# Hardware DMA for all of q, k and v, and x of three batches transposed by DMA, in a windowed-attention and gMLP kernel

## The chip, the core and the metric

The kernel runs on one core of a Trainium2 chip. A core has five engines that run side by side, each with its own in-order queue of instructions: TensorE (PE, matrix products and transposes, results in PSUM), VectorE (DVE), ScalarE (ACT), GpSimd (POOL) and SyncE (SP), which computes nothing and only issues transfers. PE's weight loads are shown as an engine of their own, PEld. Sixteen DMA engines move data between the chip's main memory and the on-chip memory SBUF. A transfer is issued from the queue of SP, of ACT (both "hardware DMA": the data keep their type) or of POOL ("software DMA", which can change the type on the way, here f32 to bf16). Engines wait for one another through semaphores.

The metric is the device time of one execution in microseconds (us).

## The reference

Attention with a sliding window of 128 and four sink tokens, for 4 batches of 8 heads, 768 positions and 64 columns, and on its result x a gMLP block with a spatial gate:

```python
scores = scale * np.matmul(q, k.transpose(0, 1, 3, 2))
is_sink = pos[None, :] < int(n_sink)                 # n_sink = 4
rel = pos[:, None] - pos[None, :]
in_window = (rel >= 0) & (rel < int(window))         # window = 128
scores = np.where(is_sink | in_window, scores, -1000000000.0)
a = softmax(scores); attn_out = np.matmul(a, v)

x = attn_out.transpose(0, 2, 1, 3).reshape(B, S, H * D)      # 4 x 768 x 512
h = gelu_tanh(x @ w_in)                              # w_in 512 x 1024
u, v = h[..., :512], h[..., 512:]
v_n = (v - mean) / np.sqrt(var + 1e-06) * g_ln       # over the 512 columns
v_s = np.einsum('ts,bsd->btd', w_sg, v_n) + b_sg[None, :, None]
return x + (u * v_s) @ w_out                         # w_out 512 x 512
```

All inputs and the output are f32; the products are made in bf16.

## The kernel before

All work is cut into steps. A step is a small function named by two or three letters with the indices of its batch, head pair and part, and it issues one instruction or a few, always on the same engine. The string STEPS (line 15) lists every step in one order, and the loop at line 475 issues them in that order; each engine's queue so holds its own steps in the order of the list and takes them strictly one after another. Semaphores between engines follow from the tiles that the steps read and write. Buffers are rings of a few tiles: a step that takes the next tile of a ring waits until the last reader of that tile is done.

The steps of the attention, for batch b and head pair p (four pairs):

- LQ, LK (lines 165, 168): load q and k of a pair, 384 KB each, from SP. LV (171): load v from POOL by software DMA, already as bf16, in pieces of 64 elements of one position; two heads at a time for batch 0, four after that.
- CQ, CK (182, 185): cast q and k to bf16 on POOL. TQ, TK (257): transpose them on PE, six matmuls each, to PSUM; EQ (263) on DVE and EK (268) on ACT copy them to SBUF.
- QK (292): scores of a group g of two 128-row tiles (three groups per pair) on PE. EX (304): exp on ACT. MK (309): the window mask, on DVE by a product with a mask tile for g = 0 and for all of batch 0, else on POOL by two selections (lines 318 and 322). KS, SK, SX: the sink tokens.
- AV (329): product with v on PE, in two halves of three row tiles; NR (354): division by the sum of weights on DVE, written to x_sb, one half of x for one pair.

The steps of the gMLP for a batch:

- XT (363): transpose 128 columns of x on PE, six matmuls; XE (369): copy them on ACT to xT, so that xT holds x transposed. Four of each for a batch, XT.b.p after both NR of pair p.
- MV (375): x @ w_in, second half of the columns, two row tiles jj at a time, eight matmuls; GV: gelu on ACT; BN, RS, Z (387 to 418): the normalization. BN runs on DVE; RS is four short steps on POOL (399 to 403); Z runs on ACT for row tiles below ZACT = 4 and on DVE for the rest.
- MU (420): first half of the columns, transposed, eight matmuls for each of four parts; GU: gelu on ACT.
- WT, WE (432, 438): w_sg transposed on PE, once. SP (441): the spatial product, six matmuls for each half hf and part dc; GT (448): times g, plus b, on DVE; GM (453): times u, on POOL.
- OU (457): product with w_out, four matmuls for each of six row tiles; RA (464): plus x, on DVE, into one of four ot buffers; ST (467): store from SP.

The remaining loads: LW (188, two halves), LWS and LWO load w_in, w_sg and w_out from POOL by software DMA as bf16. LC (199) loads the first four rows of v, g and b_sg in ten small transfers from SP, as its first.

Steps of three batches overlap: while PE works on the gMLP of batch b, the attention of b + 1 runs between, and q, k and v of b + 2 are loaded. The attention of batch 0 stands alone at the start, the gMLP of batch 3 alone at the end.

Of the kernel before, what the change touches and what calls it, by code (L numbers as in the profile page):

```python
# [20 lines left out]
LQ.1.1 LK.1.1 AV.0.1.0 EQ.0.3 EX.0.2.0 LV.1.0 AV.0.1.1 TK.0.3 NR.0.1.0 EX.0.2.1 NR.0.1.1 EK.0.3 QK.0.2.2 LWO LQ.1.2
LK.1.2 LQ.1.3 MK.0.2.0 LK.1.3 XT.0.1 EX.0.2.2 QK.0.3.1 KS.0.3 LV.1.1 MK.0.2.1 SK.0.3 EX.0.3.1 QK.0.3.0 MK.0.2.2
AV.0.2.0 SX.0.3 QK.0.3.2 MK.0.3.1 AV.0.2.1 XE.0.1 NR.0.2.0 EX.0.3.2 NR.0.2.1 EX.0.3.0 MK.0.3.2 XT.0.2 MK.0.3.0 XE.0.2
AV.0.3.1 AV.0.3.0 NR.0.3.1 NR.0.3.0 XT.0.3 XE.0.3 MV.0.0 CQ.1.0 WT.0 GV.0.0 LQ.2.0 WT.1 CK.1.0 WE.0 WT.4 WT.3 WE.1
MV.0.2 CQ.1.1 WE.4 WE.3 LQ.2.1 LK.2.0 CK.1.1 BN.0.0 TQ.1.1 GV.0.2 MV.0.1 LK.2.1 LV.2.0 BN.0.2 TK.1.1 GV.0.1 RS.0.0
# [41 lines left out]
def kernel(  # L67
# [97 lines left out]
    def LQ(b, p):  # L165
        nc.sync.dma_start(out=q32.new((b, p)), in_=q[b, 2 * p:2 * p + 2].rearrange("h (p t) d -> p h (t d)", p=128))
# [346 lines left out]
```

## Time and profile before

| | us |
|---|---|
| time, median of 3 runs | 191.5 (190.62 to 191.78) |
| the execution profiled | 191.85 |
| its span, first to last instruction | 190.1 |

| engine | busy us | share of the span |
|---|---|---|
| PE | 155.3 | 82% |
| DVE | 124.8 | 66% |
| POOL | 120.7 | 64% |
| ACT | 115.2 | 61% |

The mean granted clock of PE was 0.961 of full speed. A profile row for a group of instructions gives the line of the program, the engine, the operation, what is written and read, and the number of instructions; after the bar the busy time in us and the mean of one in ns; after the second bar the idle time of the engine just ahead of them and what ended it. In the chain of waits, the profile starts at the last instruction and goes back, at each step to what released it.

### The profile page before, as it was taken

To read this page: it belongs to the slowest core of one execution; us is meant where nothing else is said; L and a number is where in the kernel's file an instruction comes from. 1 tells how busy PE (TensorE), PEld (TensorE's weight loads), DVE (VectorE), ACT (ScalarE), POOL (GpSimd) and SP (SyncE) were. 2 spreads that over 40 slices of the span, in tenths; PEclk is the share of its full clock that TensorE was granted. 3 is DMA by queue.
4 is the path that set the end of the run, shared out by engine and by line. 5 is a ranking of instruction groups with operands and counts; after the bars stand their busy time and mean duration, and the time that the engine had idled before them with its cause. 6 is when DMAs were issued, how large, how long until landed. Compare 5 with 4: busy or idle time off the path is not lost.

```text
span 190.1 us, 3794 instructions
## 1 busy us (share of the span) xinstructions
PE 155.3 (82%) x1460; PEld 93.4 (49%) x1460; DVE 124.8 (66%) x254; ACT 115.2 (61%) x139; POOL 120.7 (64%) x192
## 2 busy tenths in 40 slices
PE   0037687630899999998999899999999999999990
PEld 0023454400657654766456466664565674455530
DVE  6524879800679598678767648775885874873670
ACT  2007589560059978578786897579698855692000
POOL 6359998100047999999899659974163992253920
PEclk9999789995599999999999999999999999999998
DMA  2999999999990791113999700043100002230053
GB/s 21 197 388 349 272 284 235 267 258 194 181 100 2 216 229 56 59 59 108 381 264 192 24 3 0 2 171 122 44 3 2 0 3 110 110 114 0 0 196 137
DMA packets 40114, 25.44 MB, mean 134 GB/s; under 512 B 26400, under 2 KB 36896, under 8 KB 40096
## 3 DMA queue, kind: packets, MB, share of 16 engines
q0 software_dynamic: 27104, 5.90, 36.9%
q1 hardware_dynamic: 12992, 19.31, 30.5%
q8 instruction: 11, 0.18, 0.4%
q14 instruction: 7, 0.06, 0.1%
HBM read 24.81 MB, written 6.29 MB: 164 GB/s over the span
## 4 chain that ended last, share of the span: by engine, by line
PE 58%; DMA 17%; POOL 15%; DVE 3%; SPq 2%; issue 1%; ACT 1%; POOLq 0%
PE mm L444 14%; DMA wsg_gated<-in_moe_w_sg_dram 13%; PE mm L461 11%; PE sc L380 10%; PE sc L424 8%; DMA k<-in_k_dram 4%; POOL q L178 4%; POOL k L178 3%; PE sc L299 3%; PE mm L255 3%; POOL wsg_gated L454 3%; PE mm L367 2%; PE mm L436 2%; PE mm L339 2%; POOL P L318 1%; POOL v_sb L174 1%
## 5 line engine op out<-in xcount | busy, mean ns | idle before, releaser
L307 ACT ACTIVATE P<-sc 128x1024 bf16<-128x1024 f32 (+1 forms) x48 | 44.1, 964 | 12.9 <-PE sc L299 11.9
L454 POOL TENSOR_TENSOR wsg_gated<-gtmp,uT 128x384 bf16<-128x384 bf16 x32 | 31.3, 987 | 11.6 <-DVE gtmp L449 10.9
L444 PE MATMUL mm<-wsgT,z 128*128 128x384 bf16 x192 | 33.9, 326 | 0.0
L449 DVE SCALAR_TENSOR_TENSOR gtmp<-mm,g_sb,b_bc 128x384 bf16<-128x384 f32 x32 | 19.4, 614 | 12.3 <-PE mm L444 11.7
L399 POOL TENSOR_SCALAR rs<-mv 128x2 f32<-128x2 f32 x12 | 2.5, 208 | 34.8 <-DVE mv L393 34.4
L385 ACT ACTIVATE vt<-sc 128x1024 f32<-128x1024 f32 x12 | 12.3, 1023 | 19.3 <-PE sc L380 19.3
L444 PEld LDWEIGHTS <-z 128*128 128x128 bf16 x192 | 17.8, 98 | 12.2 <-issue 1.6
L380 PE MATMUL sc<-w_in_sb,xT 128*128 128x512 bf16 x96 | 23.3, 388 | 0.2 <-ACT xT L370 0.2
L465 DVE TENSOR_TENSOR ot<-mm,x_sb 128x512 f32<-128x512 f32 x24 | 16.5, 688 | 10.3 <-PE mm L461 10.3
L461 PE MATMUL mm<-w_out_sb,wsg_gated 128*128 128x512 bf16 x96 | 23.2, 379 | 0.0
L424 PE MATMUL sc<-xT,w_in_sb 128*128 128x384 bf16 x128 | 22.3, 326 | 0.0
L270 ACT COPY kT<-mm 128x768 bf16<-128x768 bf16 x16 | 12.9, 803 | 14.2 <-PE mm L255 14.2
L265 DVE COPY qT<-mm 128x768 bf16<-128x768 bf16 x16 | 15.1, 948 | 8.9 <-PE mm L255 8.4
L314 DVE TENSOR_TENSOR P<-P,mask 128x1024 bf16<-128x1024 bf16 (+1 forms) x24 | 18.8, 795 | 1.3 <-ACT P L307 1.2
L339 PE MATMUL mm<-v_sb,P 128*128 128x65 bf16 x192 | 17.1, 196 | 2.5 <-DVE P L314 2.4
L255 PE MATMUL mm<-iden,q 128*128 128x128 bf16 x96 | 8.8, 237 | 12.5 <-POOL q L178 12.5
L359 DVE TENSOR_TENSOR x_sb<-mm,rcp 128x384 bf16<-128x384 f32 x32 | 17.8, 557 | 1.1
L299 PE MATMUL sc<-qT,kT 64*128 64x256 bf16 x192 | 16.4, 275 | 2.5 <-ACT P L307 1.3
L392 DVE BATCH_NORM_STATS2 st<-vt 128x6 f32<-128x512 f32 x24 | 16.2, 676 | 3.2 <-ACT vt L385 3.1
L318 POOL TENSOR_SCALAR_AFFINE_SELECT P<-P 128x512 bf16<-128x512 bf16 x24 | 15.2, 635 | 4.0 <-ACT P L307 3.8
L339 PEld LDWEIGHTS <-P 128*128 128x128 bf16 x192 | 14.8, 99 | 5.2 <-DVE P L314 2.7
L178 POOL TENSOR_SCALAR q<-q 128x768 bf16<-128x768 f32 x16 | 13.7, 860 | 4.8 <-DMA q<-in_q_dram 4.7
(61 smaller groups left out, 276.6 us busy)
## 6 DMA issues: line engine op xcount, KB each, us to landing
q<-in_q_dram SPq DMA_DIRECT2D x16, 384.0 KB
k<-in_k_dram SPq DMA_DIRECT2D x16, 384.0 KB
out_dram<-ot SPq DMA_DIRECT2D x24, 256.0 KB
v_sb<-in_v_dram POOLq DMA_DIRECT2D x6, 384.0 KB, 21.1
wsg_gated<-in_moe_w_sg_dram POOLq DMA_DIRECT2D x1, 1152.0 KB, 24.7
w_in_sb<-in_moe_w_in_dram POOLq DMA_DIRECT2D x2, 512.0 KB, 19.2
v_sb<-in_v_dram POOLq DMA_DIRECT2D x4, 192.0 KB, 14.7
w_out_sb<-in_moe_w_out_dram POOLq DMA_DIRECT2D x1, 512.0 KB, 27.6
```

What stands on the lines that cost most here:

```text
L178: nc.gpsimd.tensor_scalar(out=dst.rearrange("p t h d -> p h t d"), in0=src.rearrange("p h (t d) -> p h t d", d=Dh), scalar1=1.0, scalar2=1 ...
L299: nc.tensor.matmul(sc[:, hl, 256 * jl:256 * jl + n], kT[b, p][rows, 128 * j:128 * (j + 1)], qT[b, p][rows, 128 * j:128 * j + n], start=Tru ...
L307: nc.scalar.activation(out=pt[:, :, 0:w], in_=sc_ring[b, p, g][:, :, 0:w], func=AF.Exp, scale=scale)
L314: nc.vector.tensor_mul(pt[:, :, 0:w], pt[:, :, 0:w], m.unsqueeze(1).to_broadcast([128, 2, w]))
L339: nc.tensor.matmul(av[:, il, hl, :], P[b, p, i // 2][:, hl, 256 * (i % 2):256 * (i % 2) + 128], vb[:, h, i, :], start=first, stop=False)
L359: nc.vector.tensor_mul(xs[:, 3 * half:3 * half + 3, 128 * p:128 * (p + 1)].rearrange("p t (h d) -> p t h d", h=2), av[:, :, :, 0:Dh], rcp. ...
L380: nc.tensor.matmul(hp[:, jl, :], xT[b][:, c, 128 * j:128 * (j + 1)], w_in_sb[:, c, d_half:2 * d_half], start=(c == 0), stop=(c == KD - 1))
L424: nc.tensor.matmul(hp[:, hf, 0:NH], w_in_sb[:, c, 128 * dc:128 * (dc + 1)], xT[b][:, c, NH * hf:NH * (hf + 1)], start=(c == 0), stop=(c == ...
L444: nc.tensor.matmul(ps[:, 0:NH], z[b][:, si, 128 * dc:128 * (dc + 1)], wsgT[:, si, NH * hf:NH * (hf + 1)], start=(si == 0), stop=(si == NT ...
L449: nc.vector.scalar_tensor_tensor(out=gtmp.new((b, hf, dc)), in0=mm_ring["g", b, hf, dc][:, 0:NH], scalar=g_sb[:, dc:dc + 1], in1=b_bc[:, N ...
L454: nc.gpsimd.tensor_mul(gatedT[:, (2 * b + hf) % 3, dc, :], gtmp[b, hf, dc], uT[b][:, dc, NH * hf:NH * (hf + 1)])
L461: nc.tensor.matmul(ps, gatedT[:, (2 * b + hf) % 3, dc, 128 * tl:128 * (tl + 1)], w_out_sb[:, dc, :], start=(dc == 0), stop=(dc == KU - 1))
```

## The change

1. LV loads v of one head pair (as LQ and LK do) from SP as f32 into a new ring v32 of four tiles; a new step CV on POOL casts it into v_sb. There are 16 LV and 16 CV.
2. LC's ten small transfers are issued from ACT's queue.
3. HOLDS: the load LQ.1.0 waits until LWS, the load of w_sg, is complete.
4. For batches 1 to 3 the 12 XT and 12 XE are gone. XD.b.half, issued from SP, transposes three row tiles of x (128 partitions x 1,536 columns of bf16, 393 KB) by one DMA from x_sb to xT. xT's order of axes becomes row tile, block of columns, row. Batch 0 keeps XT and XE.
5. GM runs on DVE instead of POOL. MK of group 2 of batch 0 runs on POOL instead of DVE. ZACT is 2 instead of 4, so Z of row tiles 2 and 3 runs on DVE, and RS leaves out its last two short steps where no Z on ACT needs them.
6. Three ot buffers instead of four.
7. The list of steps is in a new order. The places around the new steps, as far as they are spoken of below, are quoted in the diff.

```diff
-IDEN LC ZERO LQ.0.0 LK.0.0 LV.0.0 LQ.0.1 LK.0.1 VSK MASK VSM CQ.0.0 CK.0.0 TQ.0.0 EQ.0.0 LQ.0.2 LV.0.1 LK.0.2 TK.0.0
...
+VSK LQ.0.0 ZERO LC LK.0.0 MASK LQ.0.1 LK.0.1 LV.0.0 LQ.0.2 LK.0.2 IDEN LV.0.1 CQ.0.0 LQ.0.3 LK.0.3 TQ.0.0 CK.0.0
...
+TK.0.2 CV.0.1 EK.0.2 MK.0.0.1 QK.0.1.0 QK.0.1.1 CQ.0.3 EX.0.1.0 KS.0.2 AV.0.0.0 SK.0.2 EX.0.1.1 LW.0 TQ.0.3 NR.0.0.0
+QK.0.2.1 AV.0.0.1 MK.0.1.0 EX.0.2.1 CK.0.3 QK.0.1.2 MK.0.1.1 LW.1 SX.0.2 TK.0.3 NR.0.0.1 EX.0.1.2 QK.0.2.2 AV.0.1.0
+MK.0.2.1 LWS EX.0.2.2 QK.0.2.0 NR.0.1.0 EX.0.2.0 LWO EQ.0.3 EK.0.3 MK.0.2.2 MK.0.2.0 XT.0.0 QK.0.3.1 KS.0.3 XE.0.0
...
+XT.0.3 XE.0.3 MU.0.0 MV.0.2 GU.0.0 LQ.1.0 LK.1.0 LV.1.0 WT.5 LQ.1.1 WT.1 GV.0.2 WE.5 LK.1.1 WT.4 MV.0.0 WE.1 LV.1.1
...
+EX.1.2.0 GT.0.1.2 AV.1.2.1 CV.2.1 NR.1.3.1 TK.2.1 SP.0.0.1 EK.2.1 NR.1.2.1 CV.2.2 GM.0.1.2 AV.1.3.0 XD.1.1 CK.2.2
+GT.0.0.1 QK.2.1.1 QK.2.1.2 OU.0.3 NR.1.3.0 EX.2.1.1 CQ.2.2 GM.0.0.1 CK.2.3 TK.2.2 EX.2.1.2 MK.1.2.0 OU.0.0 EK.2.2
+RA.0.3 CQ.2.0 AV.1.2.0 RA.0.0 ST.0.3 CV.2.3 TK.2.3 LQ.3.0 TQ.2.0 NR.1.2.0 EK.2.3 LK.3.0 OU.0.2 MK.2.1.2 ST.0.0 LV.3.0
+EQ.2.0 OU.0.1 XD.1.0 MK.2.1.1 RA.0.2 QK.2.0.2 KS.2.0 QK.2.0.0 EX.2.0.2 TQ.2.2 CQ.2.3 ST.0.2 OU.0.4 LQ.3.1 RA.0.1
...
+AV.2.3.0 MK.2.2.2 EK.3.0 GT.1.1.1 TK.3.2 QK.3.1.0 NR.2.3.0 EK.3.2 QK.3.0.2 MK.2.3.2 AV.2.2.1 GM.1.1.1 XD.2.0 EX.3.1.0
+TQ.3.2 GM.1.0.3 OU.1.5 NR.2.2.1 EX.3.0.2 EQ.3.2 AV.2.3.1 MK.3.0.2 QK.3.0.1 RA.1.5 QK.3.0.0 EX.3.0.1 OU.1.3 NR.2.3.1
+ST.1.5 EX.3.0.0 SP.1.0.1 KS.3.0 MK.3.0.1 XD.2.1 RA.1.3 QK.3.1.1 QK.3.1.2 GT.1.0.1 OU.1.4 EX.3.1.1 ST.1.3 MK.3.0.0
+SP.1.0.0 EX.3.1.2 GM.1.0.1 MK.3.1.1 RA.1.4 MV.2.0 MK.3.1.0 ST.1.4 MK.3.1.2 GT.1.0.0 GM.1.0.0 SK.3.0 MV.2.2 SX.3.0
...
+NR.3.2.0 AV.3.3.0 SP.2.0.1 GT.2.1.0 MK.3.2.2 NR.3.3.0 AV.3.3.1 GM.2.1.0 XD.3.0 AV.3.2.1 GT.2.0.1 OU.2.5 NR.3.3.1
+GM.2.0.1 OU.2.3 RA.2.5 NR.3.2.1 OU.2.4 ST.2.5 RA.2.3 XD.3.1 SP.2.0.3 RA.2.4 SP.2.0.0 GT.2.0.3 ST.2.3 ST.2.4 GM.2.0.3
+MV.3.0 GT.2.0.0 GM.2.0.0 OU.2.1 GV.3.0 OU.2.2 RA.2.1 MV.3.1 ST.2.1 RA.2.2 BN.3.0 ST.2.2 MV.3.2 GV.3.1 RS.3.0 BN.3.1
...
+HOLDS = "LQ.1.0<LWS"
...
+    v32 = Ring("v32", 4, [128, 2, NT, Dh], F32)
...
-    xT = Ring("xT", 1, [128, KD, S], BF16)
+    xT = Ring("xT", 1, [128, NT, KD, 128], BF16)
...
-    ot = Ring("ot", 4, [128, d_model], F32)
+    ot = Ring("ot", 3, [128, d_model], F32)
...
-    def LV(b, i):
-        n = 2 if b == 0 else 4
-        hs = slice(n * i, n * i + n)
-        nc.gpsimd.dma_start(out=v_sb[b % 2][:, hs, :, 0:Dh].rearrange("p h t d -> p (h t) d"),
-                            in_=v[b, hs].rearrange("h (t p) d -> p (h t) d", p=128))
+    def LV(b, p):
+        return nc.sync.dma_start(out=v32.new((b, p)).rearrange("p h t d -> p (h t) d"),
+                                 in_=v[b, 2 * p:2 * p + 2].rearrange("h (t p) d -> p (h t) d", p=128))
...
+    def CV(b, p):
+        return cast(v_sb[b % 2][:, 2 * p:2 * p + 2, :, 0:Dh], v32[b, p])
...
-            nc.sync.dma_start(out=vs32[n_sink * h:n_sink * (h + 1), :, :],
+            nc.scalar.dma_start(out=vs32[n_sink * h:n_sink * (h + 1), :, :],
...
+    MK0 = (2,)
...
-        if g == 0 or b == 0:
+        if g == 0 or (b == 0 and g not in MK0):
...
+    def XD(b, half):
+        ts = slice(3 * half, 3 * half + 3)
+        return nc.sync.dma_start_transpose(out=xT.get(b)[:, ts, :, :].rearrange("p t c i -> p (t c) i"),
+                                           in_=x_sb[b][:, ts, :].rearrange("p t d -> p (t d)"))
...
-                nc.tensor.matmul(hp[:, jl, :], xT[b][:, c, 128 * j:128 * (j + 1)],
+                nc.tensor.matmul(hp[:, jl, :], xT[b][:, j, c, :],
...
-                                 xT[b][:, c, NH * hf:NH * (hf + 1)],
+                                 xT[b][:, 3 * hf:3 * hf + 3, c, :],
...
+        if 2 * jj >= ZACT:
+            return
...
-    ZACT = 4
+    ZACT = 2
...
-        nc.gpsimd.tensor_mul(gatedT[:, (2 * b + hf) % 3, dc, :], gtmp[b, hf, dc],
+        nc.vector.tensor_mul(gatedT[:, (2 * b + hf) % 3, dc, :], gtmp[b, hf, dc],
                              uT[b][:, dc, NH * hf:NH * (hf + 1)])
...
+            done[step] = code[name](*(int(i) for i in idx))
+            if step in holds:
+                tc.add_manual_dep(done[step].ins, done[holds[step]].ins.name, after)
```

More of the change, by code (lines that the diff above doesn't have):

```diff
@@ L21 @@
[L21 to L25, printed above, removed]
@@ L207, in IDEN @@
+        nc.scalar.dma_start(out=b_bc, in_=moe_b_sg.partition_broadcast(128))
     def IDEN():
```

116 lines of the change are left out of this document (57 added, 59 removed).

## The prediction, made before the changed kernel was run

> **What bounds the kernel now.** I read the time slices first, then the chain in order of time, then the windows, then the groups by shape. The span is 190.1 us; the execution profiled took 191.85 us, so 1.75 us lie outside the span, and it stands 0.35 us above the median of the runs, 191.5.
>
> ```profile
> span 190.1 us, 3794 instructions
> ...
> PE   0037687630899999998999899999999999999990
> ...
> PEclk9999789995599999999999999999999999999998
> DMA  2999999999990791113999700043100002230053
> ```
>
> Each digit is 4.75 us. The reader sees three stages: PE partly busy to about 38 us with the DMA engines full; a hole in slices 8 to 10; then PE at 9 to the end. After the hole the granted clock is at half. The chain in order of time (start, us, what; one row per piece) names what ends the hole and carries the prices of the steps:
>
> ```profile
> 23.41 24.74 DMA wsg_gated<-in_moe_w_sg_dram
> 48.19 2.74 PE mm L436 x24
> ...
> 62.63 0.33 PE sc L299 x4
> ...
> 99.74 0.34 PE mm L255 x6
> ...
> 151.65 0.78 PE mm L367 x12
> ...
> 161.70 3.45 PE sc L380 x16
> ...
> 168.18 3.90 PE sc L424 x24
> 172.08 7.80 PE mm L444 x48
> 179.88 5.19 PE mm L461 x24
> 185.10 0.69 DVE ot L465
> ```
>
> So PE steps cost: MV 1.73, MU 1.30, SP 0.975, OU 0.865, QK 0.33, a TQ, TK or XT about 0.34 (two XT here 0.78 with a gap; the six matmuls of a TQ have the same shape). The next rows are from the timeline (start, us, engine, line, what, idle before and its releaser) and from the windows (from:to, length, busy us of PE, PEld, DVE, ACT, POOL, clock, DMA share, GB/s written).
>
> ```profile
> 0.80 2.75 SPq L201 DMA_DIRECT2D vs<-in_v_dram  x8
> ...
> 4.59 0.43 SPq L166 DMA_DIRECT2D q<-in_q_dram  x1
> ...
> 28.76 1.95 SPq L166 DMA_DIRECT2D q<-in_q_dram  x2
> ...
> 2.04 1.24 POOL L174 DMA_DIRECT2D v_sb<-in_v_dram  x1 [0.68 <-DVE v_sb L238]
> ...
> 6.59 0.09 POOL L224 MEMSET halfsel<- 64x1 f32 x1
> 11.33 0.83 POOL L178 TENSOR_SCALAR q<-q 128x768 bf16<-128x768 f32 x1 [4.65 <-DMA q<-in_q_dram]
> ...
> 21.50 0.85 POOL L178 TENSOR_SCALAR q<-q 128x768 bf16<-128x768 f32 x1
> ...
> 37.63 0.81 PE L380 MATMUL sc<-w_in_sb,xT 128*128 128x512 bf16 x3
> 38.69 1.25 PE L380 MATMUL sc<-w_in_sb,xT 128*128 128x512 bf16 x5 [0.24 <-ACT xT L370]
> 48.19 2.74 PE L436 MATMUL mm<-iden,wsg_gated 128*128 128x128 bf16 x24 [8.25 <-DMA wsg_gated<-in_moe_w_sg_dram]
> ```
> ```profile
> 48.19:185.08 136.89, 134.78 (x1224) 81.03 (x1224) 99.13 (x201) 92.94 (x112) 94.36 (x151) 0.99 0.51 94
> ```
> ```profile
> 10.00:15.00 5.00, 1.76 (x14) 1.24 (x16) 1.03 (x2) 0.80 (x1) 3.52 (x5) 1.00 1.07 386
> ...
> 50.00:55.00 5.00, 5.00 (x30) 2.74 (x29) 3.45 (x8) 1.02 (x1) 1.29 (x4) 0.78 2.80 153
> ```
>
> Stage A is batch 0's attention, from the first cast at 11.33 to MV.0.0 at 37.63, 26.3 us. After MV.0.0 (1.73 us of work) PE waits for w_sg until 48.19. Stage B, 48.19 to 185.08, is bound by PE: 134.78 us busy of 136.89, so 2.11 us of gaps. The rest, 190.1 - 185.08 = 5.0 us, is the last add and store. DVE (99.13), POOL (94.36) and ACT (92.94) all have over 37 us free in stage B. Two things can therefore shorten the kernel: PE starting stage B earlier, and less PE work in it.
>
> **The change part by part.**
>
> ```profile
> L454 POOL TENSOR_TENSOR wsg_gated<-gtmp,uT 128x384 bf16<-128x384 bf16 x32 | 31.3, 987 | 11.6 <-DVE gtmp L449 10.9
> ...
> L449 DVE SCALAR_TENSOR_TENSOR gtmp<-mm,g_sb,b_bc 128x384 bf16<-128x384 f32 x32 | 19.4, 614 | 12.3 <-PE mm L444 11.7 <-POOL wsg_gated L454 0.2
> L359 DVE TENSOR_TENSOR x_sb<-mm,rcp 128x384 bf16<-128x384 f32 x32 | 17.8, 557 | 1.1
> ...
> L178 POOL TENSOR_SCALAR k<-k 128x768 bf16<-128x768 f32 x16 | 14.5, 905 | 0.2
> ...
> L174 POOL DMA_DIRECT2D v_sb<-in_v_dram x10 | 13.2, 1321 | 1.4 <-PE mm L285 0.8 <-DVE v_sb L238 0.7
> ...
> L370 ACT COPY xT<-mm 128x768 bf16<-128x768 bf16 x16 | 12.7, 810 | 5.7 <-PE mm L367 5.7
> ...
> L416 DVE TENSOR_SCALAR z<-vt,mv,rs 128x512 bf16<-128x512 f32 x8 | 4.1, 539 | 0.9 <-POOL rs L401 0.9
> L276 DVE TENSOR_TENSOR ks_sink<-kT,halfsel 128x8 bf16<-128x8 bf16 x16 | 3.9, 288 | 0.9 <-ACT kT L270 0.9
> ...
> L314 DVE TENSOR_TENSOR P<-P,mask 128x768 bf16<-128x768 bf16 x4 | 3.1, 770 | 0.0
> ```
> ```profile
> L314 DVE TENSOR_TENSOR P<-P,mask x24: 546/691/1304, 18.2 to 149.7; 128x1024 bf16<-128x1024 bf16 x20, 128x768 bf16<-128x768 bf16 x4
> ```
>
> *First loads.* Ten small loads (LC) stand ahead of q on SP's queue; they go to ACT's, where the 3.8 us of issuing end before its first EK (about 8). The first q is then issued at about 0.8 instead of 4.59. At least these 3.8 us are won; at most 6.5, when POOL's masks would be done (they end at 6.7 now, 1.9 us of it a v load and the wait ahead of it). q now lands 6.7 us after its issue with the broadcast load of b_sg just ahead of it; without that I take 5.8. The v loads stand on SP's queue now, at about 0.45 us of issue each, less than the data of a load takes. The shift is worth its whole size as long as stage A keeps its 26.3 us: it loses four MK (4 x 0.77) on DVE, which go to POOL as two masking steps each, and four v issues on POOL (4 x 1.3), and gains four v casts there (4 x 0.9). So the last XE and MU.0.0, the new first step of stage B, come at 37.63 - 5.8 = 31.8.
>
> *Weights ahead of batch 1.* Now q and k of batch 1 and, at 28.76, of half of batch 2 go out ahead of w_in and w_sg or beside them; LQ.1.0 is to wait for LWS, and SP's queue is in order, so all of batch 1's loads stand behind it. w_sg then lands as follows. LW.0 follows CQ.0.3 on POOL, 21.50 - 5.8 + 0.85 = 16.6; batch 0's 4.7 MB and b_sg's 0.4 MB at 386 GB/s need 13.2 us from about 2, so the engines are free then too. w_in and w_sg are 4.46 MB of f32 read: 11.6 us at that rate, to about 30; I add 3 us for issue and completion: 33 (31 to 38). MU.0.0 and MV.0.2 fill PE to 34.8, so WT finds w_sg there and the hole is gone. Stage B starts 48.19 - 31.8 = 16.4 us earlier with 1.73 us more to do: **-14.7**. After the hole the clock is half: the 24 transposes of WT took 2.74 where 4 x 0.34 = 1.4 is usual, so 1.4 were lost there and perhaps 0.3 behind it. I count **-1.0**, as waits for loads may bring some of it back.
>
> *The price of the hold.* Batch 1's q and k (3.15 MB, 8.2 us at 386), its v, and w_out (1.05 MB read, 2.7 us) flow from 33.5. For v in 256-byte pieces by hardware the bounds are 386 GB/s and the 153 of the 50 to 55 row, when v by software was alone (it wrote half of what it read, 306); I take 306, 1.57 MB in 5.1 us. That is 16 us, to about 50. In that time PE has MU, MV, WT and the first SP of batch 0. It reaches TK.1.0 at 39.5, while k lands at about 39 and POOL casts it by 40.6; pairs 2 and 3 follow at 3.3 to 4 us each against PE's 4, and RS.0.1 stands behind CV.1.1 on POOL, with Z and SP.0.0.3 behind it. I count **+3.0** (0 to 6).
>
> *XT to DMA.* PE loses 12 x 0.34 = **-4.1**, all in stage B and on the chain. ACT loses 12 XE x 0.81 = 9.7. SP gains six transfers; each has to wait for all four NR of its half, and stores and batch 3's loads are queued behind it. No row shows such a transfer. The bounds are: a q load of the same 393 KB, 1.0 us at 386 GB/s plus issue; and the v loads, which like it move 1,536 pieces of 256 bytes:
>
> ```profile
> DMA to landing us min/median/max: 4.7/15.8/30.0
> ```
>
> 4.7 is a v load alone at the start, with its software issue; 15.8 is one in the queue. The transfers of batches 2 and 3 meet nearly empty engines (slices 24 to 34), so I take 5. What covers it, in PE order: from AV.3.3.0 (last for XD.3.0) to MV.3.0 stand 3 SP and 3 OU, 5.5 us, and 2 AV, less NR (0.56 and a reciprocal, some 0.75) and a GT ahead of it on DVE: 5.5. From AV.3.2.1 to MV.3.1 stand 5 OU, 2 SP and MV, 8.0, less OU, RA and NR ahead of the transfer, 2.3: 5.7. Batch 2, AV.2.3.1 to MV.2.2: 2 OU, 2 SP, 4 QK, MV, SK (four matmuls of 512 columns, like OU), 7.6, less NR and a late RA: 6.5. Batch 1, AV.1.2.0 to MV.1.0: 4 OU, 4 QK, 3 TQ or TK, MV, SK, AV, about 9.4 less 0.75: 8.6. So 5 us are hidden everywhere: **0**, and every microsecond above 5.5 to 8.6 shows three times.
>
> The Trainium skill, VectorE: DVE Perf Modes, section The three transpose paths, gives 1309 ns for a 128x128 transpose by DMA against 390 on TensorE and advises TensorE where PSUM will do; its figure for twelve blocks one after another would be an estimate of 15.7 us per half. The Trainium skill, Advanced Engine Details and Errata, X-Bar Transpose (TRN2), says instead that such transfers are as fast as ordinary ones. By the latter the term is 0, by the former it is rival 1's; no run shown has such a transfer.
>
> *Work moved between engines.* GM: 32 x 0.987 = 31.3 us leave POOL. On DVE it multiplies two bf16 tiles of 384 columns. The bounds are KS, the same operation on 8 columns (0.29), and MK's median on 1,024 and 768 (0.69); 0.35, as 384 is nearer to 8. 32 x 0.35 = 11.2. Z for two more tiles of each batch: 8 x 0.539 = 4.3 to DVE, off ACT. v casts for batches 1 to 3: 12 x 0.9 = 10.8 to POOL, against issues gone. Stage B then holds DVE 99.1 + 11.2 + 4.3 = 115, POOL at least 25 less than now (31.3 of GM and two short steps of eight RS gone, 10.8 come), ACT 10 less and eight Z, and PE 134.8 + 1.7 - 4.1 = 132. PE stays the bound, but DVE has 17 us free where it had 38, and runs in order: I count **+2.0** for PE waiting on it, net of the 2.1 us of gaps, most of which fall where POOL is full now (70 to 90 us). The new order inside xT costs nothing on PE: MV still reads 128 columns in a row, MU three such runs. Three ot buffers for four: the last store ends no later than the span, 4.3 us after the add that ends at 185.8, and three OU take 2.6; so between 0 and 1.7, **+0.5** at the end.
>
> Sum: -14.7 - 1.0 + 3.0 - 4.1 + 0 + 2.0 + 0.5 = -14.3. 191.85 - 14.3 = **177.6 us**.
>
> **The rivals.**
> 1. *The DMA transposes land late and PE waits before each batch's MV.* For it: v's 15.8 us, and a transfer behind loads or stores. Against: the engines are idle in batches 2 and 3. With a landing of L the stalls are 3L - (5.6 + 6.5 + 8.6) = 3L - 20.7. At 15.8 that is 26.7: 204 us, slower than before. At L = 11.7 the stalls eat the whole gain of 14.3; from there this rival decides. The 1309 ns of the Trainium skill, VectorE: DVE Perf Modes, The three transpose paths, point here. I give 0.17, 0.08 of it above L = 11.7.
> 2. *DVE becomes the bound.* With GM at 0.69 the DVE holds 126 us of stage B against PE's 132, and each SP of the last batch (0.975) waits for GT and GM, 1.30: 8 x 0.33 = 2.6 at the end, and I put as much again on the other three batches: 183 us. For it: MK's median, hardly less on 768 columns than on 1,024; against: DVE has attention's waits to fill in the other batches. 0.13.
> 3. *Batch 1 comes late.* If w_sg lands at 38, WT waits from 34.8 and all of batch 1's loads move by 5: +5 to +6, 183 us. For it: a landing of 24.7 us for w_sg now; against: it shared the engines with q and k. 0.12.
>
> **How the numbers follow.** Forecast 0.58, spread 172 to 183: the shift 3.8 to 6.5, the load waits 0 to 6, DVE 0 to 4 (not all at one end). With rivals 2 and 3 and the near half of rival 1 the range runs from 171 (shift 6.5, no load wait, the half clock wholly gone, a DVE term of 0: 177.6 - 0.7 - 3.0 - 0.7 - 2.0 = 171.2) to 188. About 1%, 1.9 us, is what a measurement here can tell from no change. Slower by more: the upper part of rival 1, 0.08. Within: 0.03. Faster: 0.89.
>
> **What would show it.** First cast of q at 5 to 6 us; first matmul of L424's MU at about 32; w_sg landed by then or shortly after, no 8 us hole, no half clock at 48; PE's last matmul near 171, its work in stage B near 131 us; transfers of XD landing in about 5 us and no wait of MV for xT; GM near 0.35 us on DVE. A wait of MV on the transposing DMA of several us, DVE at 9 in all slices of stage B, or w_sg landing after 38 would make the forecast wrong, each by its rival's price.

## The result and the profile after

| | before | changed |
|---|---|---|
| time, median | 191.64 us (190.62 to 192.52) | 175.55 us (174.87 to 176.9, 4 runs) |
| ratio, 95% interval | | 0.917 [0.910, 0.924] |
| the execution profiled | 191.85 us | 176.9 us |
| its span | 190.1 us | 174.8 us |
| mean granted clock | 0.961 | 0.999 |

The change makes the kernel 8.3% faster, 2 us better than the 177.6 us forecast. The execution that was profiled is the slowest of the four. The time slices of the changed kernel, 4.37 us to a digit (the last row is what the DMA engines moved, one number to a slice):

```profile
span 174.8 us, 3628 instructions
...
PE   0355697999989998999999999999999999999990
...
PEclk9999999999999999999999999999999999999999
DMA  5998999999999995459999501790310079310045
GB/s 175 277 249 240 237 178 190 209 302 302 294 309 295 310 308 115 85 156 285 307 305 295 197 6 22 165 177 0 120 60 4 0 165 199 120 60 0 6 173 188
```

The hole of three slices is gone, and with it the half clock. What is left are a first stage with PE half busy, and then PE at 9 to the end. In the next fence are the windows of stage A (first cast to the first matmul of MU.0.0) and of stage B (to the last matmul), with the columns as before, and between them stage A of the kernel before:

```profile
4.75:36.99 32.24, 22.44 (x229) 14.54 (x229) 22.39 (x40) 19.69 (x24) 19.38 (x25) 1.00 1.08 230
```
```profile
11.33:37.63 26.30, 18.40 (x228) 11.80 (x229) 19.13 (x36) 17.84 (x23) 21.47 (x22) 0.94 1.30 293
```
```profile
36.99:170.78 133.79, 131.33 (x1163) 76.20 (x1160) 116.83 (x241) 83.09 (x96) 74.96 (x116) 1.00 0.63 164
```

Three things are to be seen. Stage A begins 6.6 us earlier but is 5.9 us longer, and its DMA rate is 230 GB/s where it was 293. Stage B holds 131.33 us of PE work; the prediction had 131.4. And PE's gaps in it are 2.46 us, where the prediction allowed 7.1 (the 2.1 of before, 3.0 for batch 1's loads, 2.0 for DVE).

The timeline of the changed kernel shows the transposing DMAs of the last batch, and the matmuls that read what they write (start, us, engine, line, what):

```profile
139.67 1.44 SPq L388 DMA_TRANSPOSE xT<-x_sb  x1
...
142.72 1.42 SPq L388 DMA_TRANSPOSE xT<-x_sb  x1
```
```profile
144.66 1.89 PE L399 MATMUL sc<-w_in_sb,xT 128*128 128x512 bf16 x8
...
148.11 3.62 PE L399 MATMUL sc<-w_in_sb,xT 128*128 128x512 bf16 x16
```

MV.3.0 begins 5.0 us after XD.3.0 is issued, MV.3.1 5.4 us after XD.3.1, and neither row has a wait. No matmul waits for a transposed tile in any batch.

### The profile page after: what moved, and what is told of

Same layout as the page of the kernel before. It is cut to its first block, busy times and chain, and to the rows that moved or that the text cites. A ratio compares the mean times of both kernels' runs of the same rounds, so it can differ in the third digit from the quotient of the medians.

```text
span 174.8 us, 3628 instructions
## 1 busy us (share of the span) xinstructions
PE 153.8 (88%) x1388; PEld 90.7 (52%) x1388; DVE 142.8 (82%) x290; ACT 102.8 (59%) x119; POOL 97.9 (56%) x158
## 3 DMA queue, kind: packets, MB, share of 16 engines
HBM read 24.81 MB, written 6.29 MB: 178 GB/s over the span
## 4 chain that ended last, share of the span: by engine, by line
PE 56%; DVE 16%; POOL 14%; DMA 6%; issue 3%; ACT 1%; ACTq 1%; DVEq 0%; POOLq 0%
PE mm L466 14%; PE sc L399 10%; PE mm L483 10%; PE sc L446 7%; PE sc L310 5%; PE mm L266 4%; POOL k L182 3%; DVE P L325 3%; DMA vs<-in_v_dram 2%; DVE x_sb L370 2%; DMA q<-in_q_dram 2%; POOL P L329 2%; PE mm L350 2%; POOL q L182 2%; PE mm L296 2%
## 5 line engine op out<-in xcount | busy, mean ns | idle before, releaser
L466 PE MATMUL mm<-wsgT,z 128*128 128x384 bf16 x192 | 34.7, 326 | 0.7 <-DVE qT L276 0.4
L329 POOL TENSOR_SCALAR_AFFINE_SELECT P<-P 128x512 bf16<-128x512 bf16 x28 | 19.3, 689 | 17.7 <-ACT P L318 16.8
L471 DVE SCALAR_TENSOR_TENSOR gtmp<-mm,g_sb,b_bc 128x384 bf16<-128x384 f32 x32 | 19.4, 611 | 2.4 <-PE mm L466 2.2
L310 PE MATMUL sc<-qT,kT 64*128 64x256 bf16 x192 | 17.5, 295 | 2.5 <-ACT kT L281 1.4
L350 PE MATMUL mm<-v_sb,P 128*128 128x65 bf16 x192 | 18.6, 204 | 0.7 <-ACT exs L301 0.3
L182 POOL TENSOR_SCALAR q<-q 128x768 bf16<-128x768 f32 x16 | 14.8, 924 | 7.5 <-DMA q<-in_q_dram 7.5
L356 PE MATMUL mm<-v_sb,P 128*128 128x65 bf16 x160 | 17.4, 203 | 0.4 <-POOL P L333 0.4
L325 DVE TENSOR_TENSOR P<-P,mask 128x1024 bf16<-128x1024 bf16 x20 | 17.4, 889 | 0.0
L182 POOL TENSOR_SCALAR k<-k 128x768 bf16<-128x768 f32 x16 | 14.6, 910 | 4.2 <-DMA k<-in_k_dram 3.4
L333 POOL TENSOR_SCALAR_AFFINE_SELECT P<-P 128x256 bf16<-128x256 bf16 (+1 forms) x28 | 16.9, 603 | 0.0
L446 PEld LDWEIGHTS <-w_in_sb 128*128 128x128 bf16 x128 | 12.3, 98 | 8.3 <-issue 0.2
L451 ACT ACTIVATE uT<-sc 128x768 bf16<-128x768 f32 x16 | 12.9, 809 | 6.2 <-PE sc L446 6.2
## 6 DMA issues: line engine op xcount, KB each, us to landing
wsg_gated<-in_moe_w_sg_dram POOLq DMA_DIRECT2D x1, 1152.0 KB, 12.1
```

What stands on the lines that cost most here:

```text
L182: return nc.gpsimd.tensor_scalar(out=dst, in0=src, scalar1=1.0, scalar2=1.0, op0=ALU.mult, op1=ALU.mult)
L310: nc.tensor.matmul(sc[:, hl, 256 * jl:256 * jl + n], kT[b, p][rows, 128 * j:128 * (j + 1)], qT[b, p][rows, 128 * j:128 * j + n], start=Tru ...
L325: nc.vector.tensor_mul(pt[:, :, 0:w], pt[:, :, 0:w], m.unsqueeze(1).to_broadcast([128, 2, w]))
L329: nc.gpsimd.affine_select(out=p4[:, :, :, 0:128], in_=p4[:, :, :, 0:128], compare_op=ALU.is_ge, fill=0.0, base=0, pattern=[[0, 2], [0, 2], ...
L350: nc.tensor.matmul(av[:, il, hl, :], P[b, p, i // 2][:, hl, 256 * (i % 2):256 * (i % 2) + 128], vb[:, h, i, :], start=first, stop=False)
L446: nc.tensor.matmul(hp[:, hf, 0:NH], w_in_sb[:, c, 128 * dc:128 * (dc + 1)], xT[b][:, 3 * hf:3 * hf + 3, c, :], start=(c == 0), stop=(c == ...
```

## The experiments

Those with x and with GM take parts of the change that act in stage B, the rest the loads and stage A. The new order of the steps, the moves of Z and of batch 0's masks, and the three ot buffers were not tried by themselves.

**TensorE instead of DMA for x of batches 1 to 3.** In place of XD, two groups of six transposes and two copies by ACT for each half, in two placements:

```diff
     def XD(b, half):
-        ts = slice(3 * half, 3 * half + 3)
-        return nc.sync.dma_start_transpose(out=xT.get(b)[:, ts, :, :].rearrange("p t c i -> p (t c) i"),
-                                           in_=x_sb[b][:, ts, :].rearrange("p t d -> p (t d)"))
+        for c0 in (0, 2):
+            mm_ring.new(("x", b, half, c0))
+            ps = psb(("x", b, half, c0))
+            for n in range(NT):
+                tl, c = 3 * half + n // 2, c0 + n % 2
+                nc.tensor.transpose(ps[:, n, :], x_sb[b][:, tl, 128 * c:128 * (c + 1)], iden)
+            nc.scalar.copy(xT.get(b)[:, 3 * half:3 * half + 3, c0:c0 + 2, :],
+                           psb(("x", b, half, c0)).rearrange("p (t c) i -> p t c i", c=2))
```

The first placement:

> The six DMA transposes of x are undone alone: 12 transposes of 128 columns on PE and two copies on ACT for each half, placed some 2 us of PE work ahead of the first MV that reads them; all else as in the changed kernel. Prediction's step: PE has 72 transposes, 4.1 us, more in stage B, so the time rises by 4 to 5 us to about 180. Rival (the DMA transposes cost elsewhere, on SP's queue and the engines, what they save on PE): within 1.5 us of 175.6.

180.83 us, 0.943 [0.936, 0.949]. In this placement the ring of four PSUM buffers comes round before the products OU.0.4 and OU.0.5 are read, so RA.0.4 and RA.0.5 add what was written over them, and these rows of the output are not computed. The matmuls are the same in number, and the time is as expected; but it is the time of a kernel that leaves out a part of the result. The second placement has room in the ring:

> The x of batches 1 to 3 is transposed on TensorE again, by halves, two groups of six transposes for each half in the matmul ring at places where the ring has room, with two copies by ACT each; all else as in the changed kernel. Theory: the term of the prediction, 12 x 0.34 = 4.1 us of PE work on the chain: stage B about 137 us, 179 to 180.5 us. Rival: PE also waits for PSUM buffers or for ACT's copies before MV: 181 us or more, with PE work in stage B still about 134.5.

180.28 us, 0.940 [0.934, 0.947], 4.7 us above the changed kernel. The window of its stage B:

```profile
36.05:175.06 139.01, 135.38 (x1235) 80.39 (x1232) 115.74 (x241) 91.67 (x108) 73.80 (x116) 1.00 0.49 141
```

PE's work is 135.38 - 131.33 = 4.05 us more (the term was 12 x 0.34 = 4.1), and its gaps are 3.63 - 2.46 = 1.2 us more. The theory holds in the work and the time; stage B is 139.0 us where it had 137. ACT has 8.6 us more to do here, and of PE's waits in this stretch only 0.4 us are for the new copies.

**The transposing DMAs twice and five times.** This delays the landing and nothing else on the data path:

```diff
-        return nc.sync.dma_start_transpose(out=xT.get(b)[:, ts, :, :].rearrange("p t c i -> p (t c) i"),
-                                           in_=x_sb[b][:, ts, :].rearrange("p t d -> p (t d)"))
+        for _ in range(5):
+            nc.sync.dma_start_transpose(out=xT.get(b)[:, ts, :, :].rearrange("p t c i -> p (t c) i"),
+                                        in_=x_sb[b][:, ts, :].rearrange("p t d -> p (t d)"))
```

Five times:

> Each of the six transposing DMAs is issued five times in a row, so the last of the five lands late. Theory (the slack of the prediction holds): four more issues of 1.45 us lie ahead of the last landing, L is about 4 + 5.8 = 10, and PE waits 3L - 20.7 = about 9 us before the MV of batches 1 to 3: 183 to 187 us, with PE's waits for xT in the trace. Rival 1: the data of the five flow one after another at about 2.7 us each, L is about 14 and the time 190 to 200. Rival 2: the cover is larger than the prediction counted, since the steps between had become later on other engines: under 180 us.

264.52 us, 1.382 [1.374, 1.390]: above all three. The group of the transfers (min, median and max in ns of an issue, first and last start), then the waits of SP's queue, and PE's waits (engine, line, what it waited for: us in total, times, longest):

```profile
L389 SPq DMA_TRANSPOSE xT<-x_sb x30: 1275/1433/5394, 69.6 to 230.6; - x30
```
```profile
SPq L389 <- DMA xT<-x_sb: 54.2, 24, 3.9
```
```profile
PE sc L400 <- DMA xT<-x_sb: 65.7, 5, 14.8
```

The five write the same tile, so each waits for the one before it: 54.2 / 24 = 2.26 us behind an issue of 1.43 us (the median). One transfer of 393 KB thus takes about 3.7 us from the start of its issue to its landing in most cases; the longest issue alone took 5.39 us. Five take about 18.5 us, and both halves of a batch stand in the one queue. The run gives the landing, but it delays too much to measure the cover. So, with two:

> Each transposing DMA is issued twice. In the run with five the issues did not overlap: each waited for the one before it to land, 3.6 to 3.9 us apiece, so with two the second lands about 7.5 us after the issue of the first. Theory (the slack of 5.6, 6.5 and 8.6 us of the prediction): 3 x 7.5 - 20.7 = 1.8 us of waits for xT, time 176 to 179. Rival 1: the cover is larger, no wait for xT, 175 to 176. Rival 2: what the run with five showed is a queue that stands still (loads and stores behind the transfers) more than late tiles: 180 us or more.

195.11 us, 1.020 [1.011, 1.030]: about 2% slower than the kernel before. PE's matmuls that waited for xT:

```profile
89.61 3.46 PE L400 MATMUL sc<-w_in_sb,xT 128*128 128x512 bf16 x8 [3.57 <-DMA xT<-x_sb]
...
121.40 1.90 PE L400 MATMUL sc<-w_in_sb,xT 128*128 128x512 bf16 x8 [0.49 <-DMA xT<-x_sb]
128.34 3.60 PE L400 MATMUL sc<-w_in_sb,xT 128*128 128x512 bf16 x8 [4.17 <-DMA xT<-x_sb]
...
161.20 3.51 PE L400 MATMUL sc<-w_in_sb,xT 128*128 128x512 bf16 x8 [2.68 <-DMA xT<-x_sb]
167.84 2.76 PE L400 MATMUL sc<-w_in_sb,xT 128*128 128x512 bf16 x12 [0.55 <-DMA xT<-x_sb]
```

The waits are 11.5 us, and the eight matmuls behind each of the three long ones take 3.5 us where 1.89 is usual: a wait is paid once as a wait and once more, with 1.6 us, as half clock (the granted clock in these three stretches is 0.50 to 0.54). The window of stage B puts a sum to it:

```profile
35.74:189.87 154.13, 138.14 (x1163) 77.74 (x1160) 116.80 (x241) 83.05 (x96) 74.70 (x116) 0.94 0.63 159
```

Of 20.3 us more than in the changed kernel, 13.5 are gaps and 6.8 are PE work at a lower clock. Rival 2 had the time right (180 or more), but not the reason: 11.5 of the 16.0 us of gaps are waits for xT. The theory's 1.8 us falls: a landing is not the same for every half. XD.3.0, issued at 153.37, released MV.3.0 at 161.20, 7.8 us later; that is the 7.5 of the theory. But the half of batch 1 that is issued second, at 78.17, beside the loads of batch 3, released its MV only at 89.61, after 11.4 us.

**GM back on POOL.**

```diff
-        nc.vector.tensor_mul(gatedT[:, (2 * b + hf) % 3, dc, :], gtmp[b, hf, dc],
+        nc.gpsimd.tensor_mul(gatedT[:, (2 * b + hf) % 3, dc, :], gtmp[b, hf, dc],
```

> GM goes back from DVE to POOL, all else as in the changed kernel. Theory: the move kept POOL from filling; with 32 x 0.99 = 31.6 us back on it, POOL holds about 106 of the 133 us of stage B and DVE about 104, and PE waits a little more in batches 1 and 2: stage B 134 to 136 us, time 176.5 to 179. Rival: with half of RS's steps and the software v loads gone from POOL, GM fits there as well as on DVE: the same as the changed kernel within 0.7 us, 175 to 176.

186.16 us, 0.971 [0.963, 0.978]: 10.6 us above the changed kernel, more than either expected. The windows from 60 to 90 us of this run, and then of the changed kernel:

```profile
60.00:90.00 30.00, 25.15 (x270) 14.91 (x270) 22.85 (x42) 17.37 (x20) 28.45 (x40) 0.94 0.67 168
```
```profile
60.00:90.00 30.00, 28.99 (x320) 17.08 (x318) 27.87 (x59) 19.65 (x24) 27.70 (x40) 1.00 0.86 222
```

POOL is full there in both (28.45 and 27.70 of 30): casts of batch 2 and masks of batch 1. With GM among them PE loses 3.8 us in this stretch alone. Over stage B its gaps are 144.53 - 134.31 = 10.2 us:

```profile
34.86:179.39 144.53, 134.31 (x1163) 77.27 (x1160) 107.42 (x209) 83.09 (x95) 101.78 (x148) 0.99 0.58 155
```

The sum over stage B, 102 of 144.5 us, hides this. The list of steps was left as it is, made for GM on DVE; an order made for POOL might cost less, which wasn't tried. So 10.6 us is the price of GM on POOL in this order.

**Without the hold.**

```diff
-HOLDS = "LQ.1.0<LWS"
+HOLDS = ""
```

> The hold of LQ.1.0 on LWS is taken away alone. Prediction's step (batch 1's loads ahead of w_sg brought the hole): w_sg lands 8 to 12 us later than 34.5, near 44, WT waits from 40, the time rises by 4 to 6 us. Rival (w_sg has slack now, since its transfer takes turns with the loads at equal shares and WT begins only at 40): the time within 1 us of 175.6, w_sg before 40.

176.59 us, 0.921 [0.916, 0.926]; the interval overlaps that of the changed kernel. Batch 1's first loads go out at 17.1 us instead of 34.5, w_sg lands at 37.9 instead of 34.4, and WT, which first needs it at 38.74, doesn't wait. So the hold is not what closed the hole. What differs from the kernel before, without the hold too, is that less goes out ahead of w_sg and beside it: there q and k of all of batch 1 and of half of batch 2 were issued before it landed, here SP comes to the third q of batch 1 only at 33.1 us. The packets in the traces fit this: while w_sg was under way, SP's queue moved 3.07 MB in the kernel before, 1.15 MB in this run and nothing with the hold, and w_sg took 24.7, 16.7 and 12.1 us, about 4 us more for each MB. v of batch 1, which went beside w_sg by software before, was not set apart.

**What lengthens stage A.** Three places in the timeline of the changed kernel raise suspicion:

```profile
7.88 0.41 ACTq L211 DMA_DIRECT2D g_sb<-in_moe_g_ln_dram  x1
8.32 0.52 ACTq L212 DMA_DIRECT2D b_bc<-in_moe_b_sg_dram  x1
8.87 1.28 ACT L281 ACT_TABLE_LOAD   x1 [8.87 <-DMA vs<-in_v_dram]
10.17 0.80 ACT L281 COPY kT<-mm 128x768 bf16<-128x768 bf16 x1
```
```profile
14.03 0.68 DVE L253 TENSOR_TENSOR v_sink<-vs,headsel 32x512 bf16<-32x512 f32 x1
14.63 0.37 DVE L287 TENSOR_TENSOR ks_sink<-kT,halfsel 128x8 bf16<-128x8 bf16 x1
```
```profile
11.37 4.46 SPq L175 DMA_DIRECT2D k<-in_k_dram  x1
```

ACT issues small transfers until 8.84 us and makes its first EK at 10.17. DVE works off VSM (line 253) until 14.7, with KS.0.0 behind it. And SP, most of whose issues up to there take 0.4 to 0.8 us, is held for 4.46 us at the last k of batch 0. One more thing stands in the waits of SP's queue (line, what it waited for: us in total, times, longest):

```profile
SPq L172 <- DMA vs<-in_v_dram: 2.0, 1, 2.0
SPq L175 <- DMA k<-in_k_dram: 1.9, 1, 1.9
...
SPq L178 <- DMA vs<-in_v_dram: 1.2, 1, 1.2
```

Before it issues loads of q, k and v of batch 0, SP waits for earlier transfers to land, two of them small loads of the sink rows (vs) from ACT's queue. No data ties them together. In this trace the transfers from SP and ACT share eight semaphores, and once all are taken, each issue waits until the transfer that had its semaphore has landed. So on ACT's queue, too, the small loads stay in the way of q and k. First VSM alone, moved behind KS.0.1:

```diff
-TQ.0.1 VSM CK.0.1
...
-KS.0.1 MK.0.0.2
...
+TQ.0.1 CK.0.1
...
+KS.0.1 VSM MK.0.0.2
```

> One step is moved: VSM, eight DVE instructions that wait for the sink rows of v, comes after KS.0.1 instead of ahead of KS.0.0. Theory 1 (stage A is long because DVE stands in VSM from 7.4 to 14.6 us while KS.0.0 and EQ.0.1 wait behind it): SK.0.0 starts near 11.5 instead of 15.1, MU.0.0 near 34 instead of 37.0, the time falls by 2 to 3 us to about 173. Rival (stage A is paced by ACT's late first EK and by the loads, so DVE's wait is covered): MU.0.0 within 1 us of 37 and the time within 1 us of 175.6.

175.26 us, 0.913 [0.907, 0.919], MU.0.0 at 35.80 us. By itself this looked like 1.2 us. But six executions have the same code up to MU.0.0 (the changed kernel, both runs with TensorE, GM on POOL, XD twice and five times), and in them MU.0.0 comes at 34.86 to 36.99, with 35.9 in the middle; the first and the last:

```profile
34.86 1.53 PE L446 MATMUL sc<-xT,w_in_sb 128*128 128x384 bf16 x8
```
```profile
36.99 1.54 PE L446 MATMUL sc<-xT,w_in_sb 128*128 128x384 bf16 x8
```

So 35.80 shows no effect, and the profile of the changed kernel is at the late end. Then g_sb and b_bc, taken from ACT and issued by SP behind the last v of batch 0:

```diff
-        nc.scalar.dma_start(out=g_sb, in_=moe_g_ln.rearrange("(c p) -> p c", p=128))
-        nc.scalar.dma_start(out=b_bc, in_=moe_b_sg.partition_broadcast(128))
+    def LG():
+        nc.sync.dma_start(out=g_sb, in_=moe_g_ln.rearrange("(c p) -> p c", p=128))
+        nc.sync.dma_start(out=b_bc, in_=moe_b_sg.partition_broadcast(128))
...
-LV.0.3 TK.0.0
+LV.0.3 LG TK.0.0
```

> The loads of g and b_sg leave ACT's queue and are issued by SP behind batch 0's last v. Theory 2 (these two and the eight small ones hold up SP's issue of batch 0's q and k, LK.0.3 alone 4.5 us, and ACT's table load): ACT's table load starts near 6.5 instead of 8.9, the last k cast of batch 0 near 18.5 instead of 20.75, MU.0.0 near 35.5, the time 1 to 2 us lower. Rival (DVE in VSM gates stage A whatever the loads do): MU.0.0 and the time unchanged within 1 us.

173.62 us, 0.908 [0.903, 0.914]; first EK 7.28, MU.0.0 33.85. Since a gain of 2 or 3 us is not far outside the spread just told, the same kernel was run again:

> The kernel with g_sb and b_bc loaded by SP behind the last v of batch 0 a second time, in more rounds, because six executions with the same code for stage A put MU.0.0 anywhere from 34.9 to 37.0 us, nearly as wide as the gain read from one profile. Theory (ACT is free 2.5 us sooner and stage A ends sooner with it): first EK near 7.3, MU.0.0 33 to 34.5, time 173 to 174.7 and a ratio of 0.903 to 0.912. Rival (the first reading was luck): first EK near 7.3 but MU.0.0 at 35 or later, time 175 to 176, ratio 0.914 to 0.92.

173.85 us (173.33 to 175.09, 6 runs), and again:

```profile
7.30 0.80 ACT L283 COPY kT<-mm 128x768 bf16<-128x768 bf16 x1
```
```profile
33.56 1.54 PE L448 MATMUL sc<-xT,w_in_sb 128*128 128x384 bf16 x8
```

The last k of batch 0 is cast at 18.16 and 18.60 us in the two profiles, against 19.18 to 20.75 in the six. Both traces lie outside the range of the six: stage A ends some 2 us sooner. The time follows, 173.62 and 173.85 us against 175.55. The ratio of the second run, 0.915 [0.908, 0.923], does not tell it from the changed kernel's 0.917; the kernel before ranged from 188.83 to 193.05 us beside it. By its median this is the fastest version of the study, by about 1%.

Then everything at once: g_sb and b_bc as there, the eight loads of the sink rows from SP behind LK.0.2, and VSM split, batch 0 behind KS.0.1 and the others behind NR.0.3.1:

```diff
-            nc.scalar.dma_start(out=vs32[n_sink * h:n_sink * (h + 1), :, :],
+            nc.sync.dma_start(out=vs32[n_sink * h:n_sink * (h + 1), :, :],
...
-    def VSM():
-        for b in range(B):
+    def VSM(first):
+        for b in (0,) if first else range(1, B):
```

> g_sb and b_bc are loaded by SP behind the last v of batch 0, the eight small loads of the sink rows by SP behind k of pair 2, and VSM is split: batch 0 after KS.0.1, the other three behind the last NR of batch 0. Theory: what lengthens stage A is ACT and DVE standing in these steps; all gone, the first EK starts at about 7, KS.0.0 no longer stands behind VSM, and MU.0.0 comes at 31.5 to 33 where it was 37.0 in the changed kernel and 33.9 with the two loads alone moved. If w_sg still lands at 34, PE waits 0 to 1 for it: time 171.5 to 173. Rival: stage A is then bound by the casts on POOL and the order of loads on SP, and nothing comes beyond the two loads: MU.0.0 at 33.5 to 34.5, 173.5 to 174.5 us.

175.33 us, 0.915 [0.909, 0.921], no faster, though MU.0.0 comes where the theory has it:

```profile
31.91 1.53 PE L448 MATMUL sc<-xT,w_in_sb 128*128 128x384 bf16 x8
```
```profile
39.43 0.83 POOL L182 TENSOR_SCALAR q<-q 128x768 bf16<-128x768 f32 x1 [9.66 <-DMA q<-in_q_dram]
```
```profile
31.91:60.00 28.09, 25.02 (x211) 14.33 (x209) 23.08 (x46) 19.89 (x24) 19.00 (x29) 1.00 1.13 283
```

PE now stands 3.07 us from MU.0.0 to 60 us (the changed kernel: 0.86 us), while POOL waits 9.66 us for q of batch 1, whose load was released at 35.66, when w_sg had landed. MU.0.0 came 5.1 us earlier than in the profile of the changed kernel, w_sg 1.2 us later. If bytes ahead of w_sg are the reason, taking some away should help:

```diff
-EX.0.2.0 LWO EQ.0.3
+EX.0.2.0 EQ.0.3
...
-LV.0.3 LG TK.0.0
+LV.0.3 TK.0.0
...
-LK.1.1 WT.4
+LK.1.1 LG WT.4
...
-CV.1.1 LK.2.1
+CV.1.1 LWO LK.2.1
```

> As the run with the small loads and VSM moved (its MU.0.0 came at 31.9, but PE then stood 3.1 us in the first 28 us of stage B, mostly for batch 1's q and k), with w_out's load moved from behind w_sg to behind CV.1.1 and g_sb and b_bc to behind LK.1.1. Theory: before 35 us the DMA engines are the bound, and 1.05 MB of w_out and 0.4 MB of b_bc taken out from in front bring w_sg to 31 to 32.5 and batch 1 forward by 2 to 4 us: PE idle in that stretch under 1.2 us, time 171 to 173. Rival: batch 1 is paced by SP's queue and POOL's casts and not by the bytes ahead of it: w_sg at 34 or later or the same waits, 174.5 to 176.

177.13 us, 0.926 [0.920, 0.932]: a miss. w_sg still lands at about 34.5, and MU.0.0 comes at 34.68, though stage A's own steps are those of the run before. The rival is right in the date of w_sg, but its time is 1.1 us too low, and that pacing by SP and POOL is the reason isn't shown. Why stage A took 2.8 us longer than in the run before is open; it is more than the spread of 2.1 us between executions of one program.

Last, v of batch 0 by software DMA again:

```diff
     def LV(b, p):
+        if b == 0:
+            return nc.gpsimd.dma_start(out=v_sb[0][:, 2 * p:2 * p + 2, :, 0:Dh].rearrange("p h t d -> p (h t) d"),
+                                       in_=v[0, 2 * p:2 * p + 2].rearrange("h (t p) d -> p (h t) d", p=128))
...
     def CV(b, p):
-        return cast(v_sb[b % 2][:, 2 * p:2 * p + 2, :, 0:Dh], v32[b, p])
+        return None if b == 0 else cast(v_sb[b % 2][:, 2 * p:2 * p + 2, :, 0:Dh], v32[b, p])
```

> v of batch 0 is loaded by software DMA from POOL with the cast in it, as before the change (four issues of about 1.3 us on POOL, four casts of 0.85 away); the rest as in the changed kernel. Theory: v by hardware on SP's queue is part of what delays the last q and k of batch 0: last k cast by 19.5 where it is 20.75, MU.0.0 35 to 36, time 174 to 175. Rival 1: the small loads on ACT and VSM on DVE decide stage A: MU.0.0 36.5 to 37.5, 175.2 to 176.2. Rival 2: the software loads take descriptors and engines from q, k and the weights: w_sg after 35.5, time over 176.5.

175.07 us, 0.919 [0.909, 0.929], MU.0.0 at 35.24, last k cast at 19.46: within the spread of the six. For batch 0 it makes no difference that can be seen whether v comes by hardware or by software. One row tells more:

```profile
7.08 0.85 POOL L185 TENSOR_SCALAR q<-q 128x768 bf16<-128x768 f32 x1
```

With the issues of v ahead of it on POOL, the first cast comes at 7.08 instead of 4.75 us, and stage A ends no later. So the end of stage A does not follow the first cast.

## Why the prediction was right, and where it was lucky

The forecast was 177.6 us and -14.3 us; the profiled executions differ by 14.95. The parts, from the windows, by where the prediction put them:

| | predicted | measured |
|---|---|---|
| start of stage B against 48.19 | -16.4 (31.8) | -11.2 (36.99) |
| PE work in stage B, MV.0.0 and half clock in it | -3.4 (131.4) | -3.45 (131.33) |
| gaps of PE in stage B | +5.0 (7.1) | +0.35 (2.46) |
| from PE's last matmul to the end of the span | +0.5 | -1.0 (4.02) |
| outside the span | 0 | +0.35 (2.1) |
| sum | -14.3 | -14.95 |

*The start.* The first cast came at 4.75, a shift of 6.6 us where 5.8 was taken and 6.5 was the bound. The step that failed is "the shift is worth its whole size as long as stage A keeps its 26.3 us". It took 32.2 us in this execution, and 30.1 in the shortest of the six. The prediction looked at what POOL and DVE have to do in the stage; the loads of batch 0 it took to flow at 386 GB/s and to be in by about 15 us. From 4.4 to 21.9 us the slices show 237 to 277 GB/s. The casts on POOL show what this does, in the kernel before and then in the changed one:

```profile
22.30 1.15 POOL L178 TENSOR_SCALAR k<-k 128x768 bf16<-128x768 f32 x1
```
```profile
7.93 0.83 POOL L182 TENSOR_SCALAR q<-q 128x768 bf16<-128x768 f32 x1 [1.55 <-DMA q<-in_q_dram]
...
16.41 0.83 POOL L182 TENSOR_SCALAR k<-k 128x768 bf16<-128x768 f32 x1 [1.42 <-DMA k<-in_k_dram]
...
20.75 0.84 POOL L182 TENSOR_SCALAR k<-k 128x768 bf16<-128x768 f32 x1
```

In the kernel before, the first cast was late and the loads of the other pairs had caught up meanwhile: from the first cast to the last of k it took 22.30 - 11.33 = 11.0 us, and POOL waited for no load in them. In the changed kernel the casts wait for pair after pair, six times and 4.8 us in all, and it took 20.75 - 4.75 = 16.0. Five of the 5.9 us lie in this stretch: the first cast came forward by 6.6 us, the last by 1.6. The small loads are one part of the reason. The prediction had the 3.8 us of their issuing end before ACT's first EK at about 8; ACT was kept by them until 8.84, SP waited 3.2 us for two of them, and with g_sb and b_bc out of the way stage A ends 2 us sooner. What the rest is (28.8 to 29.1 us in those runs, against 26.3) stays open; VSM alone and v by software for batch 0 show no effect.

*The gaps.* 3.0 us for the hold and 2.0 for DVE were allowed, and 0.35 appeared. Here the hold costs nothing that can be seen: without it the gaps of stage B are at most 2.9 us, with it 2.46. The prediction counts on it to close the hole; the run without it has no hole either. Its price is tied to the start: in the run where MU.0.0 came at 31.91, where the prediction had put it, the gaps of stage B were 4.8 us, 2.4 more than in the changed kernel, and q of batch 1, held until w_sg had landed, was what POOL waited for. In the second run with g_sb and b_bc moved, with MU.0.0 at 33.56, they were 2.3. So some 2.4 of the 4.65 us too much belong to a start that did not come, and the rest was too much in any case. That the errors of 5.2 and 4.65 us cancel is in good part luck, and the prediction was luckier than its chances say. The term for w_sg itself was good: 33 forecast, 34.4 measured.

*XT to DMA.* The 4.1 us of PE work are confirmed by the run with TensorE, 4.05. The term of 0 for XD holds. A landing was taken as 5 us; by the semaphore updates in the trace, which no view prints, the six took 3.65 to 6.29 us from the start of the issue, 4.5 in the mean. The Trainium skill, VectorE: DVE Perf Modes, The three transpose paths, from which 15.7 us per half was an estimate, doesn't agree with this trace for twelve blocks in one transfer. The Trainium skill, Advanced Engine Details and Errata, X-Bar Transpose (TRN2), which has these transfers as fast as ordinary ones, agrees better: 393 KB in 3.7 us at the quickest, and the stores of 256 KB landed 3.1 us after theirs.

*The cover of XD* was given as 5.5, 5.7, 6.5 and 8.6 us. From the issues to the MV it is 5.0 and 5.4 (batch 3), 5.6 (XD.2.1 to MV.2.2) and 6.6 (XD.1.0 to MV.1.0): less by 0.3 to 2.0 us. And it was nearly used up:

```profile
78.15 4.27 SPq L388 DMA_TRANSPOSE xT<-x_sb  x1
```
```profile
84.77 1.89 PE L399 MATMUL sc<-w_in_sb,xT 128*128 128x512 bf16 x8
```

XD.1.0, beside the loads of batch 3, was held 4.27 us in its issue alone and landed after 6.29 us, at 84.44; the first weight load of MV.1.0 comes 0.3 us later. XD.2.1 landed 0.3 us ahead of its first reader, the halves of batch 3 1.2 and 1.3 us ahead. The rule 3L - 20.7 with its break-even at 11.7 us was too kind: with two transfers, L from 7.4 to 11.4, the kernel was slower than before. It lacked that L differs from half to half, that the cover is smaller, and the 1.6 us of half clock behind each long wait. Rival 1 stayed away by 0.3 us; that nothing shows of it is luck too, as the longest landing met the longest of the four covers. Its chance of a slower kernel, 0.08, came from a rule that put the limit too far out.

*DVE.* GM's median was 0.36 us, as forecast, its mean 0.47; DVE's work in stage B was 116.8 where 115 was predicted, and PE hardly waited for it. POOL's work fell by 19.4 us (94.36 to 74.96) where at least 25 were put down; a part of that is four casts of batch 1, which stood ahead of stage B before and are in it now. What the prediction didn't see is what the move is worth: it costed GM on DVE at +2.0 against gaps that stay as they were. In the new order of steps, with the casts of v on POOL, leaving GM there costs 10.6 us. The sum was right since the change does move it; a prediction for this part alone would have been wrong.

*The rest.* The end of the chain in the changed kernel:

```profile
165.59 2.60 PE mm L483 x12
...
168.22 0.70 DVE ot L487
...
168.94 2.04 DMA out_dram<-ot
...
171.10 0.69 DVE ot L487
```

An add now waits for a store that frees its buffer, but the three ot buffers cost 0.3 us of the 0.5: the last add starts 0.32 us behind PE's last matmul (170.78: 165.59 and the 5.19 us that these 24 took in the chain of before) instead of 0.02. From the end of that add to the end of the span are 3.0 us instead of 4.3. The semaphore updates show about 1 us of it: the last store landed 2.03 us after its issue, and before 2.99, as one of its sixteen parts came 0.95 us behind the others. Why is open. The half clock is gone, as predicted.

## What to carry to other kernels

An earlier first load is worth its shift only if the loads behind it come forward too: look at when the last input of a stage is cast, and compare the rate at which it is fed. Where a stage that starts earlier then needs loads that are held until something else has landed, look at both dates: a price for the wait holds for one start only. A transfer that nothing waits for may still have only a third of a microsecond to spare, so look at when it lands and not only at whether something waits. And before reading a microsecond out of one profile, look at how far the same stretch spreads over executions of identical code; here it was 2.1 us.
